# Gate loads with two neighbouring tokens per partition, summed by 64-row TensorE tiles

## The chip, the cores and the metric

The kernel runs on one core of one Trainium2 chip. The metric is the device time of that core in microseconds (us). Fast runs of one kernel agree within about 1.4%, and each run is marked fast or slow. Verdicts and ratios use fast runs only, and a kernel counts as faster or slower when it differs by more than 2%. TensorE is called PE, VectorE DVE, ScalarE ACT, GpSimd POOL and SyncE SP, as in the profile. "Half clock" means that the TensorE clock granted in the trace is 0.5 of full speed.

## The reference, cut to what matters

The first half is a gated linear recurrence with complex gates, the second a gated feed-forward block. Shapes are batch 4, heads 8, tokens 768, head size 48; the feed-forward goes from 384 to 1536 and back.

```python
mag = sqrt(a_re*a_re + a_im*a_im)
scale = minimum(mag, 0.999) / (mag + 1e-6)
for t in range(768):                         # per batch and head
    S = (a[t] * scale[t])[:, None] * S       # complex, 48 x 48
    S.real += outer(k[t], v[t])
    y[t] = q[t] @ S.real
x = y, heads side by side: (3072, 384)
out = x + sigmoid(x @ w_res) * ((gelu(x @ w_gate) * (x @ w_val)) @ w_out)
```

A running product of gates is a running sum of their logarithms and angles. That sum is what the change is about. Token t is needed only relative to the middle of its group of 256, so the kernel sums logarithms and angles over 256 tokens at a time and works on twelve such groups.

## The kernel before

A group of 256 tokens is two chunks of 128. Each chunk is loaded with one token to a partition, so each of the 8 heads gives a partition a run of 48 f32 values, which is 192 bytes. The running sum over tokens is then one 128-row f32 matmul per chunk with a triangular matrix (csl for logarithms, cst for angles):

```python
def rows(a, g, c):
    b, s = divmod(g, NS)
    t0 = (s * C + c) * 128
    return a[b, :, t0:t0 + 128, :].rearrange("h t d -> t h d")

def load_a(g):
    for nm, src in (("ar", a_re), ("ai", a_im)):
        t = lda.tile([128, C, H, D], FP, tag=nm, name=nm)
        for c in range(C):
            nc.sync.dma_start(out=t[:, c], in_=rows(src, g, c))
        T[nm, g] = t
# ... csl: logarithms
    nc.tensor.matmul(out=cs, lhsT=lmat[c], rhs=T["lm", g][:, sl], start=True, stop=True)
# ... cst: angles, plus the carry P of the groups before, then modulo one turn on VectorE
    nc.tensor.matmul(out=cs, lhsT=tmat[c], rhs=th[:, sl], start=True, stop=(s == 0))
    if s > 0:
        nc.tensor.matmul(out=cs, lhsT=ones2pi, rhs=T["P", g], start=False, stop=True)
    nc.vector.tensor_scalar(out=r, in0=cs3, scalar1=MAGIC, scalar2=MAGIC, op0=OP.add, op1=OP.subtract)
    nc.vector.tensor_tensor(out=fg[:, hs, 1, :], in0=cs3, in1=r, op=OP.subtract)
    if c == C - 1:   # the last fold of the group
        nc.vector.scalar_tensor_tensor(out=fg[:, :, 0, :], ...)
```

For most groups from 4 on, the factor M that carries the state from one group to the next is made from one row of the group's own exponentials, which small DMAs turn so that it lies across partitions (tiles dm and m). VectorE multiplies the parts when they have landed:

```python
def decay3(g):
    m = T["m2", g]
    M = mp.tile([128, H], FP, tag="M", name="M")
    nc.vector.tensor_tensor(out=M[0:DD], in0=m[0:DD, 0], in1=m[0:DD, 1], op=OP.mult)
    nc.vector.tensor_tensor(out=M[0:DD], in0=M[0:DD], in1=T["m1", g][0:DD, 0], op=OP.mult)
    T["M", g] = M
```

Groups go through the kernel in pairs. In each of five overlapped stages the gates of the next pair are summed while the attention of this pair and the output matmuls of the pair before run. A feed-forward stretch follows each. A scheduler decides the final order of instructions on every engine.

Of the kernel before, what the change touches and what calls it, by code (L numbers as in the profile page):

```python
# [28 lines left out]
def kernel(  # L29
# [27 lines left out]
    I2PI = 1.0 / (2.0 * math.pi)  # L57
# [8 lines left out]
    lmat = []  # L66
    tmat = []
    for val, dst in ((1.0, lmat), (I2PI, tmat)):
        ut = singles.tile([128, 128], FP, name="ut%d" % len(dst) + ("a" if val == 1.0 else "b"))
        make_upper_triangular(nc, ut, val=val, diag=True)  # L70
        lt = singles.tile([128, 128], FP, name="lt%d" % len(dst) + ("a" if val == 1.0 else "b"))
        nc.vector.tensor_scalar(out=lt, in0=ut, scalar1=-val, scalar2=None, op0=OP.add)
        dst.append(lt)
        dst.append(ut)
# [5 lines left out]
    for jm in range(4):  # L80
        nc.vector.tensor_copy(out=mask4[:, jm, :], in_=lmat[1])
# [41 lines left out]
    def act(**kw):  # L123
        tab(nc.scalar.activation(**kw))  # L124
# [7 lines left out]
    def load_a(g):  # L132
        for nm, src in (("ar", a_re), ("ai", a_im)):
            t = lda.tile([128, C, H, D], FP, tag=nm, name=nm)
            for c in range(C):
                nc.sync.dma_start(out=t[:, c], in_=rows(src, g, c))  # L136
            T[nm, g] = t

# [36 lines left out]
    def p1_steps(g):  # L175

        def s0():
            T["lm", g] = flat(T["ar", g])
            T["th", g] = flat(T["ai", g])
            act(out=T["lm", g], in_=T["lm", g], func=AF.Ln)  # L180

        def s1():
            T["s", g] = pS.tile([128, W], FP, tag="s", name="s")
            act(out=T["s", g], in_=T["lm", g], func=AF.Exp, scale=-1.0)
            nc.vector.tensor_tensor(out=T["th", g], in0=T["s", g], in1=T["th", g], op=OP.mult)  # L185

        def s2():
            act(out=T["s", g], in_=T["th", g], func=AF.Square)

        def s3():  # L190
            act(out=T["s", g], in_=T["s", g], func=AF.Ln, bias=1.0)

        def s4():
            lm = T["lm", g]
            nc.vector.scalar_tensor_tensor(out=lm, in0=T["s", g], scalar=0.5, in1=lm, op0=OP.mult, op1=OP.add)
            nc.vector.tensor_scalar(out=lm, in0=lm, scalar1=LNMAX, scalar2=None, op0=OP.min)  # L196

        return [s0, s1, s2, s3, s4]
# [5 lines left out]
    def cs_l(g, c):  # L204
# [5 lines left out]
        nc.tensor.matmul(out=cs, lhsT=lmat[c], rhs=T["lm", g][:, sl], start=True, stop=True)  # L210

        def ex():
            act(out=T["E", g][:, sl], in_=cs, func=AF.Exp)
            act(out=T["Ei", g][:, sl], in_=cs, func=AF.Exp, scale=-1.0)
        return ex

    def carry(g):

        s = g % NS
        if s > 0:  # L220
            P = stt.tile([128, DM], FP, tag="P", name="P")
            nc.vector.tensor_tensor(out=P, in0=T["th", g - 1][:, DM:W], in1=T["th", g][:, 0:DM], op=OP.add)
# [4 lines left out]
    def cs_t(g, c):  # L227
# [4 lines left out]
        sl = slice(c * DM, (c + 1) * DM)  # L232
        cs = psM.tile([128, DM], FP, tag="mm", padded_shape=[128, 512], name="cst")
        nc.tensor.matmul(out=cs, lhsT=tmat[c], rhs=th[:, sl], start=True, stop=(s == 0))  # L234
# [21 lines left out]
    def turn(nm, g, srcs):  # L256
        n = len(srcs)
        md = dr.tile([n, DM], FP, tag="d" + nm, name="d" + nm)
        for i, src in enumerate(srcs):
            nc.gpsimd.dma_start(out=md[i:i + 1, :], in_=src)  # L260
# [6 lines left out]
    def decay_early(g):  # L267

        ps = psM.tile([D, H], FP, tag="mm", padded_shape=[128, 512], name="dps")
        ones = lmat[1][:, 127:128]  # L270
        for i, src in enumerate((T["lm", g - 1][:, DM:W], T["lm", g][:, 0:DM])):
            for h in range(H):
                nc.tensor.matmul(out=ps[:, h:h + 1], lhsT=src[:, h * D:(h + 1) * D], rhs=ones,
                                 start=(i == 0 and h == 0), stop=(i == 1), skip_group_check=True)
# [8 lines left out]
    def decay0(g):  # L283
        turn("m1", g, [T["lm", g][0:1, 0:DM]])
# [302 lines left out]
```

## Time and profile before

| | before |
|---|---|
| time, median of 3 runs | 342.94 us (342.63 to 344.98) |
| span of the profiled run, mean granted clock | 338.6 us, 0.963 (that run took 340.38 us) |
| PE, DVE, ACT busy | 80%, 73%, 60% |
| DMA packets | 134,811 for 30.24 MB |
| first overlapped stage starts (logarithm table load) | 51.12 us |
| first feed-forward table load | 90.81 us |
| overlapped stages 1 to 5 | 39.69, 21.15, 20.09, 20.79, 19.08 us |

The table loads of ScalarE mark the stages: an overlapped stage runs from the load of the logarithm table to the load of the gelu table, and the feed-forward stretch from there to the next logarithm table. All stage times below are read that way, from the profiled runs.

The prediction shows the main views of this kernel. One more is needed later. In VectorE's timeline of the kernel before (start, length, line, operation, tiles), at the end of the second overlapped stage:

```profile
134.56 0.95 DVE L244 SCALAR_TENSOR_TENSOR fg<-fg 128x768 f32<-128x768 f32 x1
...
136.16 0.16 DVE L296 TENSOR_TENSOR M<-m_1277 96x8 f32<-96x8 f32 x1
```

The reader is to see that the product M comes after the last fold of the angles (fg), and that no wait is printed beside it.

### The profile page before, as it was taken

How to read it: one execution, taken by the hardware profiler on the slowest of the kernel's cores; microseconds unless marked ns; L12 is line 12 of the kernel's file. 1: busy time of each engine (PE TensorE's matmuls, PEld its weight loads, DVE VectorE, ACT ScalarE, POOL GpSimd, SP SyncE). 2: the span in 40 equal slices, each digit the busy share in tenths (PEclk: the TensorE clock that was granted, in tenths of full speed). 3: DMA queues.
4: the chain of work that ended last, by engine and by line, in shares of the span. 5: the costliest groups of instructions: out<-in, count | busy, mean ns of one | idle time of the engine just before them, and what ended most of it. 6: DMA issues, size and time to landing. Idle time of an engine off the chain costs nothing.

```text
span 338.6 us, 5677 instructions
## 1 busy us (share of the span) xinstructions
PE 271.1 (80%) x2148; PEld 165.0 (49%) x2148; DVE 246.3 (73%) x440; ACT 203.6 (60%) x338; POOL 59.6 (18%) x90
## 2 busy tenths in 40 slices
PE   0342644596599979999798999688999989999995
PEld 0122333564375445556444676354665556665452
DVE  0423995478997379998499996699994799855443
ACT  3356463577757795756896566967469174662530
POOL 9500800043302132110241000250002300000000
PEclk9999975589999999999999999999999999999999
DMA  9999999999999999127432610011000210002002
GB/s 142 137 146 180 182 184 183 198 178 152 163 172 167 172 164 182 47 52 69 23 96 49 120 21 2 1 48 48 3 0 3 48 46 2 2 2 93 0 2 94
DMA packets 134811, 30.24 MB, mean 89 GB/s; under 512 B 126720, under 2 KB 134784, under 8 KB 134784
## 3 DMA queue, kind: packets, MB, share of 16 engines
q1 hardware_dynamic: 103296, 23.60, 40.5%
q0 software_dynamic: 31488, 6.28, 21.6%
q8 instruction: 17, 0.28, 0.4%
q14 instruction: 10, 0.08, 0.1%
HBM read 31.32 MB, written 4.75 MB: 106 GB/s over the span
## 4 chain that ended last, share of the span: by engine, by line
PE 54%; SPq 14%; ACT 12%; DVE 10%; issue 5%; DMA 4%; POOL 0%; ACTq 0%; DVEq 0%
PE vp L437 12%; PE gp L433 12%; SPq L136 12%; PE op L457 7%; PE rp L449 3%; DMA ar<-in_a_re_dram 3%; PE tp L343 3%; PE at L350 3%; ACT L468 3%; PE tp L340 3%; ACT CS L124 2%; DVE fg L244 2%; SPq L143 2%; PE y L388 2%; PE dk L380 2%
## 5 line engine op out<-in xcount | busy, mean ns | idle before, releaser
L433 PE MATMUL gp<-xT,wg 128*128 128x512 bf16 x216 | 63.8, 378 | 7.1 <-DVE xT L424 5.1
L437 PE MATMUL vp<-xT,wv 128*128 128x512 bf16 x216 | 61.4, 379 | 0.0
L345 ACT COPY qk<-tp 96x512 bf16<-96x512 bf16 x48 | 27.9, 581 | 24.5 <-PE tp L343 11.5
L185 DVE TENSOR_TENSOR ai<-s,ai 128x768 f32<-128x768 f32 x12 | 11.4, 958 | 37.0 <-ACT s L124 25.4
L353 DVE TENSOR_TENSOR atm<-at,mask_81 128x512 bf16<-128x512 f32 x48 | 32.8, 684 | 7.0 <-PE at L350 7.0
L433 PEld LDWEIGHTS <-wg 128*128 128x128 bf16 x216 | 19.9, 97 | 23.1 <-issue 8.7
L437 PEld LDWEIGHTS <-wv 128*128 128x128 bf16 x216 | 20.3, 97 | 19.1
L147 POOL DMA_DIRECT2D v<-in_v_dram x24 | 21.7, 923 | 39.8 <-PE y L390 30.1
L210 PE MATMUL csl<-ar,lt0a 128*128 128x384 f32 x24 | 12.2, 597 | 18.7 <-DVE ar L196 18.7
L124 ACT ACTIVATE CS<-fg,hpi 128x768 bf16<-128x768 f32 x12 | 11.2, 935 | 23.2 <-DVE fg L244 23.2
L340 PE MATMUL tp<-ident,Q 128*96 128x128 bf16 x192 | 19.9, 229 | 4.8 <-DVE Q L315 3.4
L468 ACT ACT_TABLE_LOAD x18 | 23.1, 1283 | 1.0 <-PEq L571 0.7
L340 PEld LDWEIGHTS <-Q 128*96 128x96 bf16 x192 | 17.1, 129 | 12.5 <-DVE Q L315 5.7
L343 PE MATMUL tp<-ident,K 128*96 128x128 bf16 x192 | 21.9, 235 | 0.0
L346 DVE COPY qk<-tp 96x512 bf16<-96x512 bf16 x48 | 19.9, 414 | 1.4 <-ACT qk L345 1.2
L388 PE MATMUL y<-v,atm 128*128 128x48 bf16 x192 | 17.8, 188 | 3.3 <-DVE atm L353 3.1
L350 PE MATMUL at<-qk 96*128 96x128 bf16 x192 | 20.4, 228 | 0.0
L460 DVE SCALAR_TENSOR_TENSOR ot<-sg,op 128x384 f32<-128x384 f32 x24 | 13.2, 550 | 9.6 <-PE op L457 9.5
L388 PEld LDWEIGHTS <-atm 128*128 128x128 bf16 x192 | 13.5, 98 | 13.3 <-DVE atm L353 12.5
L234 PE MATMUL cst<-ai,lt0b 128*128 128x384 f32 x24 | 11.1, 544 | 9.5 <-ACT ai L124 9.2
L124 ACT ACTIVATE ar<-ar 128x768 f32<-128x768 f32 x12 | 9.7, 834 | 12.3 <-DMA ar<-in_a_re_dram 12.3
L343 PEld LDWEIGHTS <-K 128*96 128x96 bf16 x192 | 17.1, 133 | 0.0
(146 smaller groups left out, 631.0 us busy)
## 6 DMA issues: line engine op xcount, KB each, us to landing
ar<-in_a_re_dram SPq DMA_DIRECT2D x24, 192.0 KB, 6.2
ai<-in_a_im_dram SPq DMA_DIRECT2D x24, 192.0 KB, 5.1
q<-in_q_dram SPq DMA_DIRECT2D x24, 192.0 KB, 4.3
k<-in_k_dram SPq DMA_DIRECT2D x24, 192.0 KB, 4.5
out_dram<-ot SPq DMA_DIRECT2D x24, 192.0 KB, 1.9
v<-in_v_dram POOLq DMA_DIRECT2D x24, 96.0 KB, 7.1
wg<-in_moe_w_gate_dram POOLq DMA_DIRECT2D x4, 288.0 KB, 9.5
wv<-in_moe_w_val_dram POOLq DMA_DIRECT2D x4, 288.0 KB, 10.8
```

Source lines behind the costliest of these rows:

```text
L124: tab(nc.scalar.activation(**kw))
L136: nc.sync.dma_start(out=t[:, c], in_=rows(src, g, c))
L340: nc.tensor.transpose(out=tp[0:DD, j * 128:j * 128 + 128], in_=Q(x), identity=ident)
L343: nc.tensor.transpose(out=tp[0:DD, 512 + j * 128:640 + j * 128], in_=K(x), identity=ident)
L345: nc.scalar.copy(out=qk[0:DD, 0:512], in_=tp[0:DD, 0:512])
L350: nc.tensor.matmul(out=at[:, j], lhsT=qk[0:DD, 512 + j * 128:640 + j * 128], rhs=qk[0:DD, j * 128:j * 128 + 128], start=True, stop=True)
L353: nc.vector.tensor_tensor(out=atm, in0=at, in1=mask4, op=OP.mult)
L388: nc.tensor.matmul(out=ys, lhsT=st["atm", hg][:, j], rhs=V(h), start=True, stop=first)
L433: nc.tensor.matmul(out=gp, lhsT=wg[:, fi, ffi * 128:(ffi + 1) * 128], rhs=xT[:, fi, :], start=(fi == 0), stop=(fi == KD - 1))
L437: nc.tensor.matmul(out=vp, lhsT=wv[:, fi, ffi * 128:(ffi + 1) * 128], rhs=xT[:, fi, :], start=(fi == 0), stop=(fi == KD - 1))
L457: nc.tensor.matmul(out=ps, lhsT=h2[:, ffi, jj * 128:(jj + 1) * 128], rhs=wo[:, ffi, :], start=(ffi == 0), stop=(ffi == KF - 1))
L468: tab(nc.scalar.preload_act_table_set(nm))
```

## The change

Two neighbouring tokens go to one partition. They lie side by side in memory, so a run becomes 384 bytes and the gates need half as many packets (24,576 instead of 49,152 in the packet records). A chunk of 128 tokens then fills 64 partitions, with even tokens in one half of a row and odd ones in the other. Its sum is two 64-row matmuls whose masks put the tokens back in natural order. Chunk 0 uses partitions 0 to 63 and chunk 1 partitions 64 to 127, two row tiles whose matmuls start 0.01 us apart in the changed kernel's trace (69.13 and 69.14 us, below). One set of masks serves both sums: it carries the factor 1/(2 pi) that the angles need, and the exponentials after csl multiply it back (scale=TWOPI, not shown).

```diff
+    pair = singles.tile([128, 2, 128], FP, name="pair")
+    nc.gpsimd.memset(pair[0:64], -I2PI)
+    for j in range(2):
+        nc.gpsimd.affine_select(out=pair[0:64, j], in_=pair[0:64, j], compare_op=OP.is_gt, fill=0.0, base=j,
+                                pattern=[[-1, 128]], channel_multiplier=2)
 # ... rows 64 to 127 of pair: the same for chunk 1, made in tail and copied
     def load_a(g):
+        b, s = divmod(g, NS)
         for nm, src in (("ar", a_re), ("ai", a_im)):
-            t = lda.tile([128, C, H, D], FP, tag=nm, name=nm)
-            for c in range(C):
-                nc.sync.dma_start(out=t[:, c], in_=rows(src, g, c))
+            t = lda.tile([128, W], FP, tag=nm, name=nm)
+            if g in PAIRS:
+                nc.sync.dma_start(out=t.rearrange("p (h m) -> p h m", h=H),
+                                  in_=src[b, :, s * C * 128:(s + 1) * C * 128, :]
+                                  .rearrange("h (p j) d -> p h (j d)", j=2))
 # ... else as before; PAIRS is all twelve groups
+    def gate_sum(cs, g, c, x, stop):
+        if g in PAIRS:
+            ps = slice(c * 64, (c + 1) * 64)
+            xv = x.rearrange("p (h j d) -> p j h d", h=H, j=2)
+            for j in range(2):
+                nc.tensor.matmul(out=cs, lhsT=pair[ps, j], rhs=xv[ps, j], start=(j == 0), stop=(stop and j == 1))
 # ... else one 128-row matmul as before
-        nc.tensor.matmul(out=cs, lhsT=lmat[c], rhs=T["lm", g][:, sl], start=True, stop=True)
+        gate_sum(cs, g, c, T["lm", g], True)
-        nc.tensor.matmul(out=cs, lhsT=tmat[c], rhs=th[:, sl], start=True, stop=(s == 0))
+        gate_sum(cs, g, c, th, s == 0)
 # ... the carries P and the early decay sums become two half-height adds each (pair_sum)
```

More of the change, by code (lines that the diff above doesn't have):

```diff
@@ L56 @@
     EARLY = 2
-    I2PI = 1.0 / (2.0 * math.pi)
+    TWOPI = 2.0 * math.pi
+    I2PI = 1.0 / TWOPI
+    PAIRS = range(0, 12)
     LNMAX = 0.5 * math.log(0.998001)
@@ L63 @@
     make_identity(nc, ident)
-    lmat = []
-    tmat = []
-    for val, dst in ((1.0, lmat), (I2PI, tmat)):
-        ut = singles.tile([128, 128], FP, name="ut%d" % len(dst) + ("a" if val == 1.0 else "b"))
-        make_upper_triangular(nc, ut, val=val, diag=True)
-        lt = singles.tile([128, 128], FP, name="lt%d" % len(dst) + ("a" if val == 1.0 else "b"))
-        nc.vector.tensor_scalar(out=lt, in0=ut, scalar1=-val, scalar2=None, op0=OP.add)
-        dst.append(lt)
-        dst.append(ut)
+    lt = singles.tile([128, 128], FP, name="lt")
+    ut = singles.tile([128, 128], FP, name="ut")
+    make_upper_triangular(nc, ut, val=I2PI, diag=True)
+    nc.vector.tensor_scalar(out=lt, in0=ut, scalar1=-I2PI, scalar2=None, op0=OP.add)
+    tmat = [lt, ut]
+    pair = singles.tile([128, 2, 128], FP, name="pair")
+    nc.gpsimd.memset(pair, 0.0)
+    nc.gpsimd.memset(pair[0:64], -I2PI)
+    for j in range(2):
+        nc.gpsimd.affine_select(out=pair[0:64, j], in_=pair[0:64, j], compare_op=OP.is_gt, fill=0.0, base=j,
+                                pattern=[[-1, 128]], channel_multiplier=2)
+    tail = singles.tile([128, 2, 128], FP, name="tail")
+    nc.gpsimd.memset(tail, 0.0)
+    for j in range(2):
+        nc.gpsimd.affine_select(out=tail[:, j], in_=tail[:, j], compare_op=OP.is_gt, fill=I2PI, base=j - 128,
+                                pattern=[[-1, 128]], channel_multiplier=2)
+    nc.gpsimd.tensor_copy(out=pair[64:128], in_=tail[64:128])
+    one = singles.tile([128, 1], FP, name="one")
+    nc.vector.memset(one, 1.0)
     hpi = singles.tile([128, 1], FP, name="hpi")
@@ L80 @@
     for jm in range(4):
-        nc.vector.tensor_copy(out=mask4[:, jm, :], in_=lmat[1])
+        make_upper_triangular(nc, mask4[:, jm, :], val=1.0, diag=True)
     twice = singles.tile([D, 2, D], FP, name="twice")
@@ L132, in load_a @@
     def load_a(g):
+        b, s = divmod(g, NS)
         for nm, src in (("ar", a_re), ("ai", a_im)):
-            t = lda.tile([128, C, H, D], FP, tag=nm, name=nm)
-            for c in range(C):
-                nc.sync.dma_start(out=t[:, c], in_=rows(src, g, c))
-            T[nm, g] = t
+            t = lda.tile([128, W], FP, tag=nm, name=nm)
[3 more added lines that the diff above has]
+                                  .rearrange("h (p j) d -> p h (j d)", j=2))
+            else:
+                for c in range(C):
+                    nc.sync.dma_start(out=t[:, c * DM:(c + 1) * DM].rearrange("p (h d) -> p h d", h=H),
+                                      in_=rows(src, g, c))
+            T[nm, g] = t
+    def gate_sum(cs, g, c, x, stop):
+        if g in PAIRS:
+            ps = slice(c * 64, (c + 1) * 64)
+            xv = x.rearrange("p (h j d) -> p j h d", h=H, j=2)
+            for j in range(2):
+                nc.tensor.matmul(out=cs, lhsT=pair[ps, j], rhs=xv[ps, j], start=(j == 0), stop=(stop and j == 1))
+        else:
+            nc.tensor.matmul(out=cs, lhsT=tmat[c], rhs=x[:, c * DM:(c + 1) * DM], start=True, stop=stop)
     def load_q(g):
@@ L177, in s0 @@
         def s0():
-            T["lm", g] = flat(T["ar", g])
-            T["th", g] = flat(T["ai", g])
+            T["lm", g] = T["ar", g]
+            T["th", g] = T["ai", g]
             act(out=T["lm", g], in_=T["lm", g], func=AF.Ln)
@@ L209, in cs_l, with pair_sum @@
         cs = psM.tile([128, DM], FP, tag="mm", padded_shape=[128, 512], name="csl")
-        nc.tensor.matmul(out=cs, lhsT=lmat[c], rhs=T["lm", g][:, sl], start=True, stop=True)
+        gate_sum(cs, g, c, T["lm", g], True)
         def ex():
-            act(out=T["E", g][:, sl], in_=cs, func=AF.Exp)
-            act(out=T["Ei", g][:, sl], in_=cs, func=AF.Exp, scale=-1.0)
-        return ex
+            act(out=T["E", g][:, sl], in_=cs, func=AF.Exp, scale=TWOPI)
+            act(out=T["Ei", g][:, sl], in_=cs, func=AF.Exp, scale=-TWOPI)
+        return ex
+    def pair_sum(out, nm, g):
+        for ps, t in ((slice(0, 64), T[nm, g]), (slice(64, 128), T[nm, g - 1])):
+            tv = t.rearrange("p (h j d) -> p j h d", h=H, j=2)[ps]
+            nc.vector.tensor_tensor(out=out[ps], in0=tv[:, 0], in1=tv[:, 1], op=OP.add)
     def carry(g):
@@ L221, in carry @@
             P = stt.tile([128, DM], FP, tag="P", name="P")
-            nc.vector.tensor_tensor(out=P, in0=T["th", g - 1][:, DM:W], in1=T["th", g][:, 0:DM], op=OP.add)
+            if g in PAIRS:
+                pair_sum(P.rearrange("p (h d) -> p h d", h=H), "th", g)
+            else:
+                nc.vector.tensor_tensor(out=P, in0=T["th", g - 1][:, DM:W], in1=T["th", g][:, 0:DM], op=OP.add)
             if s > 1:
@@ L231, in cs_t @@
             T["fg", g] = pE.tile([128, C * H, 2, D], FP, tag="fg", name="fg")
-        sl = slice(c * DM, (c + 1) * DM)
         cs = psM.tile([128, DM], FP, tag="mm", padded_shape=[128, 512], name="cst")
-        nc.tensor.matmul(out=cs, lhsT=tmat[c], rhs=th[:, sl], start=True, stop=(s == 0))
+        gate_sum(cs, g, c, th, s == 0)
         if s > 0:
@@ L259, in turn @@
         for i, src in enumerate(srcs):
-            nc.gpsimd.dma_start(out=md[i:i + 1, :], in_=src)
+            dst = md[i:i + 1, :]
+            nc.gpsimd.dma_start(out=dst.rearrange("r (h d) -> r h d", h=H) if len(src.shape) == 3 else dst, in_=src)
         m = mp.tile([128, n, H], FP, tag=nm, name=nm)
@@ L269, in decay_early @@
         ps = psM.tile([D, H], FP, tag="mm", padded_shape=[128, 512], name="dps")
-        ones = lmat[1][:, 127:128]
-        for i, src in enumerate((T["lm", g - 1][:, DM:W], T["lm", g][:, 0:DM])):
+        if g in PAIRS:
+            parts = [pS.tile([128, H, D], FP, tag="r", name="dsum")]
+            pair_sum(parts[0], "lm", g)
+        else:
+            parts = [x.rearrange("p (h d) -> p h d", h=H) for x in (T["lm", g - 1][:, DM:W], T["lm", g][:, 0:DM])]
+        for i, x in enumerate(parts):
             for h in range(H):
-                nc.tensor.matmul(out=ps[:, h:h + 1], lhsT=src[:, h * D:(h + 1) * D], rhs=ones,
-                                 start=(i == 0 and h == 0), stop=(i == 1), skip_group_check=True)
+                nc.tensor.matmul(out=ps[:, h:h + 1], lhsT=x[:, h], rhs=one, start=(i == 0 and h == 0),
+                                 stop=(i == len(parts) - 1), skip_group_check=True)
         m = mp.tile([D, H], FP, tag="me", name="me")
@@ L283, in decay0 @@
     def decay0(g):
-        turn("m1", g, [T["lm", g][0:1, 0:DM]])
+        row = T["lm", g][0:1].rearrange("p (h j d) -> p j h d", h=H, j=2)[:, 0] if g in PAIRS else T["lm", g][0:1, 0:DM]
+        turn("m1", g, [row])
     def decay1(g):
```

## The prediction

> **What bounds the kernel now.** I read the page's slices first, to see where stages with different limits lie, then the chain that ended last, then the timelines at its turning points. The slices (8.47 us each):
>
> ```profile
> PE   0342644596599979999798999688999989999995
> PEclk9999975589999999999999999999999999999999
> DMA  9999999999999999127432610011000210002002
> ```
>
> There are two regimes. To about 60 us (seven slices) PE is half idle and the DMA engines are full; from about 90 us PE is nearly full, DMA stays full to about 135 us and then hardly works. The chain says the same:
>
> ```profile
> PE 54%; SPq 14%; ACT 12%; DVE 10%; issue 5%; DMA 4%; POOL 0%; ACTq 0%; DVEq 0%
> PE vp L437 12%; PE gp L433 12%; SPq L136 12%; PE op L457 7%; PE rp L449 3%; DMA ar<-in_a_re_dram 3%; PE tp L343 3%; PE at L350 3%; ACT L468 3%; PE tp L340 3%; ACT CS L124 2%; DVE fg L244 2%; SPq L143 2%; PE y L388 2%; PE dk L380 2%
> ```
>
> SPq L136 plus L143 plus "DMA ar" is about 17% and lies wholly before 60.3 us: the chain in order of time is nothing but load issues until one gate tile lands. ScalarE's timeline there (start, length, line, op, idle before and its releaser):
>
> ```profile
> 52.41 0.84 ACT L124 ACTIVATE ar<-ar 128x768 f32<-128x768 f32 x1
> 53.33 0.58 ACT L345 COPY qk<-tp 96x512 bf16<-96x512 bf16 x1
> 60.33 0.84 ACT L124 ACTIVATE ar<-ar 128x768 f32<-128x768 f32 x1 [6.42 <-DMA ar<-in_a_re_dram]
> ```
>
> This is the logarithm of group 5, waiting 6.42 us for its gate; behind it, in ScalarE's order, stand the attention copies, so PE stops too. In the list of waits no other compute wait over 6 us after 50 us is for a load. Later loads are early, so **faster loads pay only up to here**.
>
> In the later stages the gate sums stand in a dense stretch of PE between two groups of output matmuls:
>
> ```profile
> 173.33 0.81 PE L234 MATMUL cst<-ai,ut0b 128*128 128x384 f32 x2
> 173.97 0.81 PE L234 MATMUL cst<-ai,lt0b 128*128 128x384 f32 x2
> 174.62 0.81 PE L236 MATMUL cst<-P,ones2pi 128*128 128x384 f32 x2
> 175.26 0.81 PE L234 MATMUL cst<-ai,ut0b 128*128 128x384 f32 x2
> 175.91 0.81 PE L236 MATMUL cst<-P,ones2pi 128*128 128x384 f32 x2
> ```
>
> Each line is one f32 instruction (two records); starts are 0.645 us apart, its cost in a stream. The other sum, csl, costs the same but has PE idle behind it:
>
> ```profile
> 164.81 0.81 PE L210 MATMUL csl<-ar,ut0a 128*128 128x384 f32 x2
> 168.08 2.11 PE L457 MATMUL op<-wo,h_1432 128*128 128x384 bf16 x12 [2.46 <-ACT Ei L124]
> ```
>
> [...] I counted its packet records by queue and size: while weights (768-byte packets) load at about 39 to 57 us, the load queue q1 gets 590 packets in 3 us and the weights 573, against 3,000 in 3 us for q1 alone. So beside weights a gate packet costs a turn, whatever it carries. [...] The records give a median of 15 ns for 192 bytes and 65 ns for 1,536 bytes (stores). [...]
>
> **The change, part by part.**
>
> *Gate loads.* 49,152 packets of 192 bytes become 24,576 of 384. Cost of a new packet by the line through the two medians: 15 + 192 x (50/1344) = 22 ns, an estimate, against 2 x 15. I put it at 20 to 25 ns.
>
> The front is then rescheduled in three pieces. a) Gates 0 to 3 (16,384 packets, now 8,192) compete with all twelve v loads (12,288 packets); together the engines take about 1,000 packets per us. They land by about 30.7 us (VectorE's first use of the last ones); with half as many, heavier packets, and v issued some 4 us later because GpSimd first builds two f32 matrices and four masks by itself (about 15 instructions of 0.2 to 0.3 us), I get about 24 us. b) q and k of groups 0 and 1 are unchanged; k of group 0 landed at 35.17 us, which released the weights. It moves to about 31. c) Weights then run from about 35 instead of 39 us. Behind them stand gates 4 and the real part of 5: before, 6,144 packets, the last some 4,100 at 195 per us (21 us). After, 3,072 packets at about 180 turns per us (a turn of 83 ns grows to some 88): 17 us, so 35 + 17 = 52 instead of 60.3. **Gain about 8 us.** The engines must follow: from the trigonometric table load at 34.93 us to 60.33 ScalarE's chain took 25.4 us, 6.4 of it this wait. From a load at about 28 to 29 us it reaches the same point at 48 to 50, so it isn't much behind the data. The compiled order also puts group 4's logarithm after more attention copies, so these no longer queue behind the wait. I take 8 to 10, say 9.
>
> *Gate sums.* 24 csl and 24 cst instructions become 48 and 48, each with 64 rows: 48 x 0.645 = 31 us more of PE if nothing overlaps. Per stage: 4 + 4. Could tiles overlap? In the compiled order the two halves of one chunk use the same rows and are adjacent; the next chunk uses the other 64. Only the seam can overlap, and between most cst pairs stands a 128-row P sum. At best a quarter is won.
> - Stage before the first attention: 5 us of PE; the front is bound by loads and has slack. About 0 to 1, inside the figure above.
> - First overlapped stage (60 to 91 us): PE is on the chain and half-clocked at first, so csl costs 2 x 1.3 + 2 x 0.65 = 3.9 and cst 2.6; dps falls from 16 to 8 instructions, half of 1.53 us, -0.8; VectorE gets up to four more adds of 0.47. Part lies beside other waits: **+4**.
> - The next three (116, 164, 210 us): csl's extra 2.6 us falls into the idle 2.5 us shown above: free. cst's 2.6 us delays the last two output groups. The new VectorE order no longer puts the third output step before the last fg in two of them, so Sin and the table load needn't move; PE enters the feed-forward about 2.6 us later, where it had waited 0.6 to 1.5 us: **+1.4 each, +4.2**.
> - The last (257 us): its chain goes csl, Exp, a transposing transfer, fg. csl leaves only 0.4 us idle there: **+2**.
>
> *VectorE.* Eight carry sums become two half-height adds of the same length: 8 x 0.47 = 3.8 us, mostly in the feed-forward stages where it waits for PE. **+0.5.** Issue of gate DMAs halves (24 instead of 48 instructions), already in the front figure.
>
> Sum: -9 + 4 + 4.2 + 2 + 0.5 = +1.7. I take off some 3 us: the reordering that frees attention from the wait, a higher PE clock if PE idles less near 50 to 60 us, and possible seam overlap. 342.94 - 1.3 gives about **341.5 us**.
>
> **Rivals.**
> R1, *loads are all that matters*: the PE cost hides and 9 to 12 us stay: 331 to 334. For it: PE idles 0.4 to 2.5 us around the later sums. Against it: PE is 54% of the chain and at "9" in most later slices.
> R2, *PE takes over*: no tile overlaps, all cst and half the csl cost stays, front gain only 5: 342.94 - 5 + 15 = 353. For: dense cst stretches. Against: csl's idle time, and ScalarE and VectorE bound parts of these stages.
> R3, *the longer packet is no cheaper*: if 384 bytes cost 30 ns, gates gain nothing alone and beside v; but the turn beside the weights still carries twice the bytes. Gain about 5: 346. [...] Against: the 1,536-byte median is far below eight times 15 ns.
> R4, *row tiles run side by side*: the added sums then cost only a quarter: about 336.
>
> **Range and chances.** The two terms are near equal and opposite, each uncertain by 3 to 4 us, and the new order of all engines may add 2 to 3 either way. Hence 334 to 349. Faster by 2% means below 336.1: R1, or R4 with a good front: 0.2. Slower means above 349.8: much of R2: 0.1. The rest 0.7.
>
> **What would show it.** Page, DMA part: 24,576 fewer packets, same bytes. ScalarE's timeline: group 5's logarithm starts at 50 to 53 us, with a wait under 3 us (front right); at 56 or later, R3. Packet records: 384 bytes at 20 to 25 ns alone. PE's timeline at the later sums: starts 0.645 us apart within a chunk, less at a seam only if tiles overlap. Stages: the stretch from table load to feed-forward table load of the second to fourth grows by 0 to 2 us; the fully covered csl leaves no idle before the first output group. I am wrong if the first feed-forward starts (86 us before) at the old time, or if a later stage grows by over 3 us.

## The result, and the profile after

The changed kernel takes 357.99 us (median of 4 runs, 354.06 to 362.42; three are fast, the one of 362.42 us is slow). Ratios here are the mean time of one kernel's fast runs over the mean of the other's in the same rounds, so they are not quite the ratio of the medians. The ratio to the kernel before is 1.039, with a 95% interval of 1.029 to 1.049: slower. The profiled run of the changed kernel is a fast one of 355.7 us at a mean clock of 0.903.

Where the 17.1 us between the two profiled spans went, in us:

| | before | after | difference |
|---|---|---|---|
| start to first overlapped stage | 51.12 | 46.49 | -4.6 |
| first overlapped stage | 39.69 | 48.51 | +8.8 |
| second | 21.15 | 26.01 | +4.9 |
| third | 20.09 | 21.96 | +1.9 |
| fourth | 20.79 | 22.07 | +1.3 |
| fifth | 19.08 | 23.98 | +4.9 |

The profiled run of the kernel before is its quickest on record, so the spans differ by 2 us more than the medians do (15.1 us). The differences add up to 17.2; the feed-forward stretches between them changed little (25.28, 26.35, 26.61, 25.56 us before and 25.24, 26.90, 26.26, 26.04 after).

**The loads did what was expected.** The queue of the gate loads, from the page of the changed kernel (queue: packets, MB, share of 16 engines' time):

```profile
q1 hardware_dynamic: 78336, 23.60, 30.9%
```

These are 24,960 packets fewer for the same bytes, and the share fell from 40.5%. A gate packet of 384 bytes took a median of 22 ns where nothing else was loaded, one of 192 bytes 15 ns (35 and 28 ns beside other loads), so doubling the run saved about a quarter of the time. Beside the weights the two queues still went packet for packet: 536 gate packets and 527 weight packets in 3 us, as 590 and 573 before. ScalarE's timeline of the changed kernel at the logarithms of groups 4 and 5:

```profile
48.16 0.85 ACT L138 ACTIVATE ar<-ar 128x768 f32<-128x768 f32 x1
...
53.14 0.84 ACT L138 ACTIVATE ar<-ar 128x768 f32<-128x768 f32 x1 [4.13 <-DMA ar<-in_a_re_dram]
```

Group 5's logarithm starts at 53.14 instead of 60.33 us and waits 4.13 us for its gate instead of 6.42.

**Then the clock stays low.** The 40 slices of the changed kernel's page (8.89 us each):

```profile
PE   0508668979599797999799999798999989999995
PEclk9967655555999998999989999999999999999999
DMA  9999999999954565126442220011000201002002
```

PE's granted clock is at 5 from the sixth to the tenth slice, where before it had only two such slices. In the records the half clock lasts from 37.6 to 88.8 us, 51.2 us in one piece, against 47.1 to 71.0 before. PE's own row is no lower meanwhile than it was before. (The 9 of the first slices can't be relied on: the first clock record comes at 13.8 us, and the eight csl records at 10.30 us took 2.94 us, those at 15.49 us, at full clock by the records, 1.57. In the kernel before the first record comes at 40.2 us. The mean clocks count the time before it as full, so they can't be compared between runs.)

PE's timeline of the changed kernel in the first overlapped stage, some of the gate sums (two records to an f32 instruction):

```profile
55.31 2.93 PE L166 MATMUL csl<-ar,pair 64*128 64x384 f32 x4
58.17 0.66 PE L385 MATMUL tp<-ident,Q 128*96 128x128 bf16 x4
...
69.13 1.01 PE L166 MATMUL csl<-ar,pair 64*128 64x384 f32 x1
69.14 1.01 PE L166 MATMUL cst<-ai,pair 64*128 64x384 f32 x1
69.93 0.84 PE L166 MATMUL csl<-ar,pair 64*128 64x384 f32 x1
...
70.57 1.48 PE L166 MATMUL csl<-ar,pair 64*128 64x384 f32 x2
```

Two things can be read here. Four records, one chunk, take 2.86 us to the start of the next work. And csl and cst, which use different rows, start within 0.01 us of each other: the tiles do run side by side. The cst record at 69.14 even starts before the csl records at 69.93 and 70.57 (the second half of that chunk), which belong to instructions ahead of it in the compiled order.

**The second stage.** PE's timeline of the changed kernel there:

```profile
119.62 2.95 PE L166 MATMUL csl<-ar,pair 64*128 64x384 f32 x16
124.83 2.11 PE L502 MATMUL op<-wo,h 128*128 128x384 bf16 x12 [2.26 <-ACT Ei L138]
...
131.33 1.55 PE L166 MATMUL cst<-ai,pair 64*128 64x384 f32 x4
132.81 0.91 PE L275 MATMUL cst<-P,ones2pi 128*128 128x384 f32 x2
133.66 1.55 PE L166 MATMUL cst<-ai,pair 64*128 64x384 f32 x4
```

All eight csl instructions together take 2.95 us, as if they were half as many, and PE still waits 2.26 us behind them. A chunk of cst with its P sum takes 133.66 - 131.33 = 2.33 us, where the kernel before took 1.29 (two steps of 0.645). VectorE's timeline of the changed kernel at the end of that stage:

```profile
134.54 0.16 DVE L341 TENSOR_TENSOR M<-m 96x8 f32<-96x8 f32 x1
139.69 0.16 DVE L341 TENSOR_TENSOR M<-m 96x8 f32<-96x8 f32 x1 [4.98 <-DMA m<-dm]
139.77 0.55 DVE L281 TENSOR_TENSOR fg<-cst,r 128x384 f32<-128x384 f32 x1
```

Here M has moved ahead of the fg instructions, and VectorE stands still for 4.98 us until the small transfer lands. The chain that ended last, in order of time (start, length, what), runs near its start in the changed kernel through exactly this wait:

```profile
136.85 2.75 DMA m<-dm
139.85 0.48 DVE fg L281
140.38 3.62 PE op L502 x12
```

It does not reach back beyond 130 us, so it says nothing about the earlier stages.

### The profile page after: what moved, and what is told of

It is laid out like the page before. It is cut to its first block, busy times and chain, and to the rows that moved or that the text cites. A ratio compares the mean times of both kernels' runs of the same rounds, so it can differ in the third digit from the quotient of the medians.

```text
span 355.7 us, 5789 instructions
## 1 busy us (share of the span) xinstructions
PE 301.5 (85%) x2212; PEld 174.4 (49%) x2212; DVE 253.7 (71%) x448; ACT 203.8 (57%) x338; POOL 62.5 (18%) x104
## 4 chain that ended last, share of the span: by engine, by line
PE 44%; DVE 8%; ACT 4%; issue 4%; DMA 2%; POOL 1%; DVEq 0%; ACTq 0%
PE gp L478 11%; PE vp L482 11%; PE op L502 8%; PE rp L494 3%; PE tp L385 2%; PE tp L388 2%; PE at L395 2%; DMA m<-dm 2%; PE cst L166 1%; PE y L433 1%; DVE fg L281 1%; DVE r L280 1%; ACT L513 1%; DVE fg L283 1%; PE dk L425 1%
## 5 line engine op out<-in xcount | busy, mean ns | idle before, releaser
L478 PE MATMUL gp<-xT,wg 128*128 128x512 bf16 x216 | 62.8, 379 | 4.4 <-DVE xT L469 3.3
L502 PE MATMUL op<-wo,h 128*128 128x384 bf16 x288 | 53.7, 340 | 9.3 <-ACT Ei L138 6.6
L138 ACT ACTIVATE h<-gp 128x512 bf16<-128x512 f32 x72 | 42.7, 597 | 32.9 <-PE gp L478 32.6
L485 DVE SCALAR_TENSOR_TENSOR h<-h,vp 128x512 bf16<-128x512 bf16 x72 | 48.4, 680 | 16.4 <-PE vp L482 16.2
L166 PE MATMUL cst<-ai,pair 64*128 64x384 f32 x96 | 37.0, 607 | 8.4 <-ACT ai L138 8.2
L502 PEld LDWEIGHTS <-h 128*128 128x128 bf16 x288 | 28.5, 101 | 31.4 <-issue 13.1
L398 DVE TENSOR_TENSOR atm<-at,mask 128x512 bf16<-128x512 f32 x48 | 32.8, 684 | 13.7 <-PE at L395 13.5
L166 PE MATMUL csl<-ar,pair 64*128 64x384 f32 x96 | 28.0, 597 | 12.6 <-DVE ar L227 12.6
L166 PEld LDWEIGHTS cst<-ai,pair 64*128 64x128 f32 x96 | 15.8, 223 | 23.1 <-ACT ai L138 9.4
L216 DVE TENSOR_TENSOR ai<-s,ai 128x768 f32<-128x768 f32 x12 | 11.4, 956 | 21.2 <-ACT s L138 21.2
L166 PEld LDWEIGHTS csl<-ar,pair 64*128 64x128 f32 x96 | 13.8, 220 | 21.0 <-issue 13.6
```

The source lines that it names most:

```text
L138: tab(nc.scalar.activation(**kw))
L166: nc.tensor.matmul(out=cs, lhsT=pair[ps, j], rhs=xv[ps, j], start=(j == 0), stop=(stop and j == 1))
L398: nc.vector.tensor_tensor(out=atm, in0=at, in1=mask4, op=OP.mult)
L478: nc.tensor.matmul(out=gp, lhsT=wg[:, fi, ffi * 128:(ffi + 1) * 128], rhs=xT[:, fi, :], start=(fi == 0), stop=(fi == KD - 1))
L485: nc.vector.scalar_tensor_tensor(out=h2[:, ffi, :], in0=h2[:, ffi, :], scalar=0.5, in1=vp, op0=OP.mult, op1=OP.mult)
L502: nc.tensor.matmul(out=ps, lhsT=h2[:, ffi, jj * 128:(jj + 1) * 128], rhs=wo[:, ffi, :], start=(ffi == 0), stop=(ffi == KF - 1))
```

## The experiments

The theory after this reading was that the added sums cost more than their length in two ways: 64-row matmuls alone don't bring the clock up, which makes the first stage long; and the scheduler's new order puts VectorE behind a small DMA in the second and fifth. The rivals were that the loads themselves delay something, that changing between 64-row and 128-row matmuls is the cost, or that the added PE time alone explains it. Before each table of numbers stands what was expected, as it was recorded. Within one set of runs the kernel before was timed on the same chip (343.25 us in the first set, 344.44 and 344.09 in the next two, 344.95 in the last).

### The loads alone

`e1_loads_only`: paired loads, but the sums of the kernel before. The tokens are in the wrong order, so the result is wrong on purpose.

```diff
-    PAIRS = range(0, 12)
+    LOADP = range(0, 12)    # read by load_a
+    SUMP = range(0, 0)      # read by gate_sum, carry and decay
```

> Paired gate loads, but the sums of the kernel before on them (its result is wrong on purpose: the rows are taken as if tokens stood in natural order). The compiled order on VectorE and ScalarE is that of the kernel before but for a few start-up instructions. Theory A (the loads alone gain what the front showed, 4.6 us at the second logarithm table, 7.2 us at group 5's logarithm, and all of the loss is in the sums): 335 to 338 us, later stages as long as before to 0.5 us. Rival B (faster loads only move the wait to another place, so nothing of it survives to the end): 342 to 344 us.

Measured: 336.86 us, ratio 0.980 (0.974 to 0.987). The first feed-forward table load comes at 83.57 us, 7.2 us earlier than before. The loads are not the cause of the loss; they gain some 6.4 us at the end (336.86 against 343.25). Group 5 still waits for its gate:

```profile
53.79 0.84 ACT L139 ACTIVATE ar<-ar 128x768 f32<-128x768 f32 x1 [8.17 <-DMA ar<-in_a_re_dram]
```

That is ScalarE's timeline of this experiment. The landing sets the start of this logarithm at 53 to 54 us, with or without the new sums.

### The sums alone

`e2_sums_only`: the loads of before, the new sums (wrong on purpose as well).

```diff
-    PAIRS = range(0, 12)
+    LOADP = range(0, 0)
+    SUMP = range(0, 12)
```

> Loads of the kernel before, paired 64-row sums on them (wrong result on purpose). The compiled order on all engines is that of the changed kernel. Theory A (parts add up): changed kernel plus the lost front gain, 362 to 366 us; first overlapped stage again about 9 us longer than before, second and fifth about 5 us longer, third and fourth 1 to 2. Rival B (the loss of the first overlapped stage comes from where the earlier loads put it in time, not from the sums): 352 to 356 us, that stage within 2 us of before.

Measured: 364.95 us, ratio 1.059 (1.049 to 1.068). The two parts add: the ratios of the fast runs multiply to 0.980 x 1.059 = 1.038, and the changed kernel has 1.039. So the total shows no interplay of loads and sums. The sums cost 10.2 us up to the first feed-forward (101.05 against 90.81 us), then 4.2, 3.3, 1.3 and 4.9 us in the four later stages. The first stage by its own marks is only 3.0 us longer, not the 9 expected, because its first mark moved too (58.36 us); so what is lost in it is counted up to the first feed-forward here. The half clock is there again, though the page's clock row hides it: the first clock record comes at 78.6 us, and the csl chunk at 63.17 us takes 2.92 us.

### The same instructions over 128 rows

`e3_full_height`: the mask of each chunk is padded with 64 rows of zeros, so that each 64-row matmul becomes a 128-row one. The number of matmuls, and the order of instructions on VectorE and ScalarE, are those of the changed kernel. The result is right.

```diff
-            ps = slice(c * 64, (c + 1) * 64)
+            # full = [pair with rows 64..127 zero, tail with rows 0..63 zero]
-                nc.tensor.matmul(out=cs, lhsT=pair[ps, j], rhs=xv[ps, j], ...)
+                nc.tensor.matmul(out=cs, lhsT=full[c][:, j], rhs=xv[:, j], ...)
```

> Changed kernel, but each gate sum runs with all 128 rows, the other half of the stationary matrix being zero: same number of matmuls, same result, same compiled order on VectorE and ScalarE, no 64-row tiles. Theory A (64-row matmuls leave TensorE at half clock from 38 to 89 us): half clock ends by about 72 us, the first overlapped stage is 3 to 6 us shorter; csl of later stages takes 5.2 us instead of 2.9 but stays hidden; a chunk's cst with its P sum takes 1.94 instead of 2.33 us, so 1 us less in each later stage: 350 to 354 us. Rival B (the clock has nothing to do with the tiles): half clock lasts as long as in the changed kernel, csl is dearer: 358 to 364 us.

Measured: 348.88 us, ratio 1.014 (1.006 to 1.023), some 9 us less than the changed kernel, although none of these sums runs beside another now (the eight csl instructions of the second stage take 5.32 us, against 2.95). The first feed-forward comes at 86.97 instead of 95.00 us. Of the later stages only the third and the fourth are shorter by the 1 us expected (20.87 and 21.28 us); the second took 27.07 and the fifth 23.94. PE's timeline of this experiment in the first overlapped stage:

```profile
55.52 2.87 PE L166 MATMUL csl<-ar,pair 128*128 128x384 f32 x4
58.19 0.63 PE L385 MATMUL tp<-ident,Q 128*96 128x128 bf16 x4
...
62.49 1.51 PE L166 MATMUL csl<-ar,pair 128*128 128x384 f32 x4
63.84 0.39 PE L385 MATMUL tp<-ident,Q 128*96 128x128 bf16 x4
```

At 55.5 us a chunk takes 2.67 us, nearly the 2.86 of the changed kernel. At 62.5 us the clock is up, and it takes 1.35 us; in the changed kernel the chunk at 64.51 us still takes 2.85. The half clock lasts from 40.3 to 60.8 us here, and returns for 6.8 us at 71.0. The two kernels side by side in the stretch up to the second table load of that stage (windows of one core: length, then busy time and count of records for PE, PEld, DVE, ACT and POOL, then granted clock, DMA share and GB/s), first the changed kernel:

```profile
46.49:80.28 33.79, 26.75 (x160) 16.87 (x160) 17.50 (x30) 14.89 (x27) 8.96 (x13) 0.50 1.20 183
```

and this experiment:

```profile
48.78:73.35 24.57, 19.23 (x160) 14.03 (x160) 17.24 (x30) 14.53 (x26) 7.64 (x11) 0.71 1.14 188
```

The same 160 PE records are 7.5 us shorter, and VectorE and ScalarE have the same work. In PE's timeline of the second stage one sees what the changes between tile shapes cost:

```profile
123.01 1.45 PE L166 MATMUL cst<-ai,tail 128*128 128x384 f32 x4
124.30 0.81 PE L275 MATMUL cst<-P,ones2pi 128*128 128x384 f32 x2
124.94 1.45 PE L166 MATMUL cst<-ai,pair 128*128 128x384 f32 x4
```

A chunk with its P sum takes 1.93 us, 0.40 less than the 2.33 of the changed kernel with its two changes of shape. By these two numbers a change costs about 0.2 us, an estimate.

In the first stage the 64-row sums of the changed kernel stand in seven groups between 128-row work, so the shape changes 14 times. At half clock leaving a chunk costs 2.86 - 2.67 = 0.19 us. Entering one costs 0.13: from the attention matmuls before the second chunk to the chunk it is 59.61 - 59.05 = 0.56 us there and 59.47 - 59.04 = 0.43 here. The pair is 0.32 us at half clock and 0.40 at full clock, so seven pairs are 2.2 to 2.8 us of the 8.0. The rest I put down to the clock, an estimate by difference; e4 below tests a part of it.

### What lifts the clock

`p1_clock`: a separate kernel with nothing but four trains of f32 matmuls on PE, with some 15 us of VectorE work between them (its output is meaningless; it was run once, so its state is unknown).

```diff
+ a_low_only: 28 matmuls over rows 0..63
+ b_full:     28 matmuls over rows 0..127
+ c_low, c_high: 28 pairs, rows 0..63 and rows 64..127 in turn
+ d_mixed:    30 matmuls, two over rows 0..63, then one over all
```

> A probe by itself (its output is no answer to the task): four trains of f32 matmuls of 384 columns with some 14 us of VectorE work between them: 28 on rows 0 to 63 only, 28 with all 128 rows, 28 pairs on rows 0 to 63 and 64 to 127 side by side, and ten times two of 64 rows and one of 128. Theory A (64-row matmuls do not lift TensorE's clock): the first train runs at half clock throughout, 1.29 us an instruction; the second goes over to 0.645 us after 3 to 8 us; the third, if rows are what counts, as the second; the fourth late or not at all. Rival B (any dense train lifts the clock): the first speeds up after 3 to 8 us like the second.

PE's timeline of the probe:

```profile
3.48 36.17 PE L66 MATMUL a_low_only<-x,ut 64*128 64x384 f32 x56 [3.48 <-DMA x<-in_q_dram]
55.04 20.03 PE L66 MATMUL b_full<-y,ut 128*128 128x384 f32 x56 [15.39 <-DVE y L62]
...
96.55 0.48 PE L66 MATMUL c_low<-y,ut 64*128 64x384 f32 x1
...
127.59 44.40 PE L66 MATMUL d_mixed<-y,ut 64*128 64x384 f32 x60 [16.05 <-DVE y L62]
```

The 64-row train takes 36 us for 56 records, 0.64 us each: half clock to its end, however busy PE is. (This is read from the records' length, since the first clock record comes at 58.5 us. That 64-row records as such aren't slower is seen in the second stage above, where the four of a chunk take 1.48 us.) The 128-row train is at half clock for about 3.7 us and then takes 0.32 us a record. The two tiles side by side are at full clock after some 6 us (records of 0.48 us instead of 0.84). The mixed train, in which two of three instructions have 64 rows, stays at half clock for all its 44 us; it also changes shape between them, so it does not show the effect of the rows alone. The first three trains do: the rows that work at one time count, not only the time in which PE is busy. Idle time shows as well: the second train ended at full clock, and after 15.39 us without PE work the third began with records of 0.84 us.

### The product M after the last fold

`e4_m_last`: the changed kernel with one more order rule for the scheduler. It takes no wait away and gives the right result.

```diff
-            nc.vector.scalar_tensor_tensor(out=fg[:, :, 0, :], ...)
+            T["fold"] = nc.vector.scalar_tensor_tensor(out=fg[:, :, 0, :], ...)
 # in decay3
-        nc.vector.tensor_tensor(out=M[0:DD], in0=m[0:DD, 0], in1=m[0:DD, 1], op=OP.mult)
+        i = nc.vector.tensor_tensor(out=M[0:DD], in0=m[0:DD, 0], in1=m[0:DD, 1], op=OP.mult)
+        tc.add_manual_dep(i.ins, T["fold"].ins.name, order, reason="after the last fold")
```

> Changed kernel, but VectorE's product M, which waits 5.0 us (second overlapped stage) and 3.7 us (fifth) for a small transfer with the rounding of the phases behind it, is ordered after the last fold of the phases. Theory A (its place in VectorE's order is what these two stages lose): second stage about 4 to 5 us shorter, fifth 3 to 5 us shorter, 349 to 352 us. Rival B (the doubled sums on TensorE set the end of these stages): 356 to 358 us.

Measured: 351.77 us, ratio 1.025 (1.017 to 1.033). The second stage fell from 26.01 to 23.21 us and the fifth from 23.98 to 21.76, less than the 4 to 5 and 3 to 5 us expected. VectorE's timeline of this experiment in the second stage:

```profile
137.43 0.56 DVE L280 TENSOR_SCALAR r<-cst 128x384 f32<-128x384 f32 x1 [0.44 <-PE cst L275]
...
141.86 0.16 DVE L341 TENSOR_TENSOR M<-m 96x8 f32<-96x8 f32 x1
```

No wait stands before M any more; what VectorE waits for near the end of the stage is cst, for about half a microsecond. The first stage has no such M, and its end moved by only 1.0 us (94.02 against 95.00).

That stage holds a test of the clock which nobody planned. PE has the same instructions in the same order there as in the changed kernel, and up to the fourth csl chunk it is 0.91 us behind it. But here the half clock ends at 71.4 us, in the changed kernel at 88.8; why is not shown. From that chunk to the second table load of the stage, first the changed kernel (windows as above):

```profile
69.13:80.28 11.15, 8.62 (x48) 4.74 (x46) 6.40 (x11) 3.23 (x8) 4.72 (x7) 0.50 1.36 159
```

and this experiment:

```profile
70.04:78.18 8.14, 5.66 (x48) 3.14 (x46) 6.40 (x11) 3.23 (x8) 3.87 (x6) 0.91 1.46 152
```

The tiles, their changes of shape and the work of VectorE and ScalarE are the same, and the stretch is 3.0 us shorter, nearly all of it PE time. So the clock by itself is worth these 3.0 us. After the table load the half clock comes back (78.3 to 85.1 and 88.5 to 91.9 us), past the end of the changed kernel's, and 1.1 us of the 3.0 are lost again.

### The two remedies together, and tiles side by side

`e5_full_m_last` is e3 and e4 together. `e6_side_m_last` is e4 with the 64-row tiles kept, but both chunks of cst issued next to each other, so that their tiles overlap (two chunks take 1.73 us in the second stage, where one alone took 1.55 in e4) and, where both chunks have a P sum, the shape changes half as often:

```diff
-        gate_sum(cs, g, c, th, s == 0)
-        if s > 0:
-            nc.tensor.matmul(out=cs, lhsT=ones2pi, rhs=T["P", g], start=False, stop=True)
+        for c in range(C):
+            gate_sum(both[c], g, c, th, s == 0)
+        for c in range(C):
+            if s > 0:
+                nc.tensor.matmul(out=both[c], lhsT=ones2pi, rhs=T["P", g], start=False, stop=True)
```

> Changed kernel with both edits tried singly: sums with all 128 rows (349 us) and M after the last fold (352 us, against 358). Theory A (clock and M's place are separate causes): gains add, 9 + 6: 342 to 345 us; fifth and second overlapped stages 2 to 3 us over the kernel before. Rival B (they are one cause, since M waits longer where TensorE is late): 347 to 349 us.

> 64-row tiles as in the changed kernel, M after the last fold, and the phase sums of a group's two chunks issued together so that both row tiles run side by side. Theory A (the later stages still lose 1 to 2.7 us each to cst's serial 64-row pairs): second to fifth stage come to within 0.7 us of the kernel before; the first overlapped stage still at half clock: 343 to 347 us. Rival B (VectorE's order, not TensorE, sets what is left): no gain over M last alone, 350 to 353 us.

| | us, median | ratio to before (95%) | first feed-forward | stages 2 to 5 |
|---|---|---|---|---|
| e5 | 341.10 | 0.989 (0.983 to 0.994) | 86.7 | 21.85, 20.79, 21.26, 22.58 |
| e6 | 346.61 | 1.007 (1.003 to 1.011) | 93.1 | 21.84, 21.78, 21.91, 19.30 |

Together the two remedies take the kernel from 358 us to just under the time of before. e6 brings the second and fifth of the later stages within the 0.7 us expected of those of before (21.15, 20.09, 20.79, 19.08), the third and fourth only within 1.7 and 1.1, so side by side the tiles are cheap there. In the fifth the M rule helps the kernel before as well (16.89 us in b1 below), and beside that e6 is still 2.4 us over. In the first stage the half clock still lasts to 84 us, and the first feed-forward comes only 0.9 us earlier than in e4. That is no test of the changes of shape there: in this order too the 64-row sums of that stage stand in seven groups, so all 14 changes remain.

### Fewer groups in pairs

`e7_six_full_m_last` is e5 with pairs for groups 0 to 5 only, whose gates load in the crowded front. `v2_0145` and `v3_45` go further. `b1_before_m_last` is the control: the kernel before with the M rule of e4 and nothing else.

```diff
-    PAIRS = range(0, 12)
+    PAIRS = range(0, 6)        # e7
+    PAIRS = (0, 1, 4, 5)       # v2; carries between a paired and a plain group are added by halves
+    PAIRS = (4, 5)             # v3; the two groups whose packets take turns with the weights
```

> Only groups 0 to 5 loaded in pairs (those that lie before or beside the weights), sums with all 128 rows there, natural order after that, M after the last fold. Theory A (later groups' loads are hidden anyway): third to fifth stage as in the kernel before, front and first stage as with full height (first feed-forward table at 87 us), 339 to 342 us, a little faster than the kernel before. Rival B (later loads matter too, through the queue): 343 us or more.

> Control: the kernel before with nothing but M ordered after the last fold. Theory A (the early place of M costs the kernel before only in its fifth stage, where VectorE waits 2.4 us for it): fifth stage about 2 us shorter, others unchanged, ratio to the kernel before 0.993 to 0.995, so that most of the 1.9% of the six-group version is due to the loads. Rival B (M's order is all that version gained): ratio 0.985 or less.

> The six-group version, but groups 2 and 3 in natural order again: their sums are those of the first overlapped stage, which then has no doubled matmuls. Theory A (a doubled sum costs more there, about 3.4 us, than 2,048 fewer packets in the first 30 us gain): ratio 0.972 to 0.98. Rival B (the loads of groups 2 and 3 set the front): first feed-forward table later than the 88.1 us of the six-group version, ratio 0.983 to 0.99.

> The six-group version, but only groups 4 and 5 in pairs, those whose packets take turns with the weights'. Theory A (the front gain is made mostly beside the weights, 4 to 5 of 7 us): group 5's logarithm at 55 to 57 us against 60.3 before, ratio 0.977 to 0.985. Rival B (it is made in the first 30 us): logarithm at 58 us or later, ratio as the control's, 0.99 or more.

| | us, median | ratio to before (95%) | first feed-forward |
|---|---|---|---|
| e7 | 338.00 | 0.981 (0.977 to 0.985) | 88.1 |
| b1 | 343.05 | 0.993 (0.989 to 0.998) | 91.9 |
| v2 | 336.77 | 0.979 (0.975 to 0.983) | 85.4 |
| v3 | 335.71 | 0.975 (0.969 to 0.981) | 87.5, in a slow run |

All four are right in their results. The M rule alone is worth 0.7% in the kernel before; there it helps only the fifth stage (19.08 to 16.89 us; the second to fourth took 1.1 to 1.3 us longer in its profiled run, from the rule or from the run). v3 is the fastest of all: 1.9% under b1 by the means of the fast runs, which is what the pairs of two groups bring. Its group 5 logarithm starts at 57.44 us, in a slow run; 55 to 57 was expected. Its interval reaches just over the 2% line, so it can't be called faster by that rule with certainty, and v2 and v3 can't be told apart. Both beat the kernel before and the changed one.

### Partners for the 64-row sums

`d1_partner`: the changed kernel, in which every sum of groups 0 to 3 gets a second 64-row matmul in the other rows, into a tile that nobody reads. Both are put into the program at high priority, which is a second change. The result stays right.

```diff
+            if g < 4:
+                dum = psM.tile([128, DM], FP, tag="mm", padded_shape=[128, 512], name="dum")
+                with tc.high_priority():
+                    for j in range(2):
+                        nc.tensor.matmul(out=dum, lhsT=pair[po, j], rhs=xv[po, j], start=(j == 0), stop=(j == 1))
+                        nc.tensor.matmul(out=cs, lhsT=pair[ps, j], rhs=xv[ps, j], start=(j == 0), stop=(stop and j == 1))
+                return
```

> The changed kernel, in which for groups 0 to 3 only (the front and the first overlapped stage) every 64-row sum gets a partner of the same size in the other 64 rows, into a spare PSUM tile that nobody reads. The result stays right, the sums stay 64-row tiles with all their switches to and from 128-row matmuls, and PE gets more instructions, not fewer. Only the number of rows that work at one time goes up; the scheduler also moves a few instructions of the front. Theory A, the clock decides the first overlapped stage: the half-clock stretch ends by about 62 us, as with full-height sums, instead of 89 us, and the first feed-forward table load comes at 87 to 91 us instead of 95.0; the end at about 350 to 354 us against 358.0. Theory B, the switches between tile shapes decide it: the stretch may shorten, but the table load stays at 94 us or later and the end at 357 us or more. If the clock stays half to about 89 us, two 64-row tiles side by side do not count as full height inside this kernel, against the probe, and A is in doubt.

Measured: 367.32 us as the median of four runs, two of which are slow; the fast ones took 364.22 and 360.84. The clock row of its page (9.06 us a slice):

```profile
PEclk9985965995889989999989999999999999999999
```

The clock did what theory A says: in the records the long half-clock stretch is 17.1 us (47.7 to 64.7) instead of 51.2, followed by one of 10.2 us from 81.8. The time did not: the first feed-forward came at 101.3 us, and the first overlapped stage took 48.65 us, as long as with the low clock. By its letter theory B came true, but the added matmuls and their priority moved the scheduler's order, so the times are no test of it. The front ended at 52.64 instead of 46.49 us, and from 63.6 to 75.0 us PE ran partners and sums almost without attention work between them, while VectorE stood idle for 6.67 us. So this run shows that two 64-row tiles at a time lift the clock inside the kernel too, and it doesn't show what that alone is worth: a higher clock didn't pay in this order. The exact split of the 8 us between clock and shape changes stays open. What is shown is that 128-row masks remove them, with VectorE and ScalarE in the same order, and, by e4's trace, that the clock alone takes 3.0 us in one stretch of the stage.

## Why the prediction was wrong

**Right: the loads.** "Gain about 8 us", then "say 9": the loads alone brought the first feed-forward forward by 7.2 us, and group 5's logarithm to 53.14 us. The start is a hair above the 50 to 53 us named, and its wait of 4.13 us is longer than the 3 us named, since ScalarE was less behind than I took it to be. The packet cost of 20 to 25 ns was 22, and the turns beside the weights were as counted.

**Right, with more than was thought: csl in the later stages.** It was predicted to be free, and PE waits 2.26 us behind it. The prediction thought that "Only the seam can overlap", since the two halves of one chunk use the same rows. In the trace all eight instructions overlap as two columns of four (2.95 us), because matmuls of free rows start ahead of earlier ones, as the cst record at 69.14 us does before the csl records at 69.93 and 70.57. That one with 64 rows takes as long as one with 128 was the prediction's estimate; the half-clocked chunks show it (2.93 us here, 2.87 in e3). Rival R4 was right about this for csl, yet it had PE's clock against it.

**Wrong: the first overlapped stage, "+4".** The working doubled csl and cst at the old clock, "half-clocked at first", and then took off "some 3 us" partly for "a higher PE clock if PE idles less". The sign of that term is what failed. Against the loads alone, the sums cost 95.00 - 83.57 = 11.4 us up to the first feed-forward. With 128-row masks they cost 86.97 - 83.57 = 3.4 us, close to the +4 that the working gives if the clock isn't hurt. The other 8.0 us come with the 64-row tiles: a half clock to 88.8 us instead of 60.8, which cost 3.0 us in one stretch where e4 tests it alone, and 14 changes of shape, some 2.2 to 2.8 us. The prediction knew the clock as a matter of an idle PE only, an estimate then; the probe shows that much (half clock again after 15.39 us of idle), but not that alone. It had no term for a change of shape, and the trace of before has no 64-row sums on which to see one.

**Wrong: the second stage.** "The new VectorE order no longer puts the third output step before the last fg", so "Sin and the table load needn't move": +1.4 was predicted, +4.9 came. The order was read as far as the output steps and not as far as M, which had moved ahead of fg. M last gives 2.8 us back, which leaves 2.1; with the tiles side by side as well, 0.7. That rest is cst, whose 2.6 us turned out as 4 x (2.33 - 1.29) = 4.2 us of PE time here, where all four chunks have a P sum.

**Wrong: the last stage, "+2".** It came to +4.9, and M last gives 2.2 back. The third and fourth stages cost 1.9 and 1.3 for the predicted 1.4 each. Only two of their four chunks have a P sum and two chunks ran side by side, so cst took about 2.3 us more of PE, near the 2.6 predicted.

In sum, -9 + 4 + 4.2 + 2 + 0.5 - 3 became -7.2 for the loads, +11.4 for the sums up to the first feed-forward, and 4.9 + 1.9 + 1.3 + 4.9 after it: +17.2, against spans that differ by 17.1. R2 was nearest in size, at 353 us, but its mechanism, tiles that never overlap, isn't what happened.

## What to carry to other kernels

Before trading one 128-row matmul for two 64-row ones, ask what else keeps the array's clock up: in the probe an f32 mix in which 64-row matmuls dominate ran at half clock for all its 44 us of dense work, and 64-row matmuls alone for 36 us; and zero rows in the mask can be cheaper than small tiles (348.88 us against 357.99). A changed instruction order must be read down to the smallest instruction that waits for a DMA, since a 0.16 us product held VectorE for 4.98 us here. And a layout that pays only where its packets take turns with other traffic should be used only there: two of twelve groups gave more than all twelve (335.71 us against 341.10).
